# Transposing the queries and keys of the last sentence by DMA, not on TensorE, in a fused window-attention and mixture-of-experts kernel

## The chip, the cores and the metric

The kernel runs on one core of a Trainium2 chip. Its engines work side by side, each through its own instruction stream in order: TensorE (PE; loading its weights is shown apart as PEld), VectorE (DVE), ScalarE (ACT), GpSimd (POOL) and SyncE (SP). The metric is the device time of one execution in microseconds: 206.28 us, the median of three runs (205.09 to 207.0).

## The reference

Eight sentences of 576 positions, eight heads of 64. Attention looks back over a window of 64 positions; its output, averaged over the positions, picks one expert for the whole sentence, and a two-layer network of that expert is applied to every position.

```python
B, H, S, D = 8, 8, 576, 64
scores = q @ k^T / sqrt(D);  mask: 0 <= pos_q - pos_k < 64
attn   = softmax(scores);    x = (attn @ v) as [B, S, H*D = 512]
e      = argmax(x.mean(axis=1) @ w_gate)              # one of 8 experts per sentence
gate   = softmax(...)[e]
out    = gate * (relu(x @ w1[e]) @ w2[e])             # w1 512 x 1024, w2 1024 x 512
```

## The kernel before

Everything is written out as one list of steps, `OPS`: each entry is a letter, perhaps a letter for the engine (a for ACT, d for DVE, m for a PSUM tile out of the shared pool `ps_m`), and a number. A loop at the end of the kernel (L559 to L589) calls the function for each entry in turn, so that the list sets the order of the instructions on every engine, and of the DMA issues on each queue. An engine runs ahead of another as far as data and buffers allow. Sentences, heads and chunks are counted from 0.

*Attention.* A sentence has five units: 5b to 5b+3 are its four pairs of heads over positions 0 to 511 (a main unit), 5b+4 is the tail, positions 512 to 575 of all heads. Sentence 7 has the units 35 to 39. The steps of a unit:

- Q loads q or k of a whole sentence (`load_qk`, L104 to L112; Q14 and Q15 are sentence 7): one DMA on POOL's queue that casts to bf16. Partition p gets the positions 4p to 4p+3 of all heads, so that a piece of 256 elements is contiguous. t loads the tail of q and k (`load_tail`).
- T transposes on TensorE (`unit_tp`, L216 to L235): for a main unit 16 matmuls against the identity, 64 x 128 each, into a PSUM tile; for the tail 8.
- U copies the transposed queries out of PSUM into a tile `qt` (`unit_q`), k the keys into `kT` (`unit_kt`), on ACT or DVE. There are two `kT`, for even and odd sentences.
- S is the scores (L259 to L279), E the exp (ACT), K the mask (DVE), l the row sums by a matmul with ones, A the values (TensorE), n and R the reciprocal of the sums by ln and exp (ACT), X the normalisation (DVE).
- L loads v in tiles of 128 positions, V shifts a copy of it by 64 partitions (DVE).

*Gate.* g, j, G: after a sentence's last X a product on DVE, a small matmul (j, L394) and an argmax; P loads the index into a register of POOL, and W loads the expert's weights, four quarters of 512 KB (4b and 4b+1 are w1, 4b+2 and 4b+3 are w2, POOL's queue). Three weight buffers take turns; where the same expert lies in the buffer already, a load is skipped at run time.

*Experts.* c is the next of 144 chunks of TensorE's work, 18 a sentence: eight of w1 (`ph`, L465) and one of w1's tail (L472), eight halves of w2 (`po`, L524) and one of w2's tail (L533). A chunk is 8 matmuls over 512 columns, or 16 over 256. Chunk 18b is the first of sentence b; the chunk 18b+10 is the first to read the quarter W 4b+3. r empties a chunk's PSUM tile (ra on ACT, rd on DVE), B and D transpose the tail between the layers, O stores a result on POOL's queue, o on SP's. Stores run behind by up to 16 buffers.

*Queues.* All loads but the first two of q and k (SP) and the gate's matrix go through POOL's one DMA queue, at most eight under way; a load of that queue waits for the landing of the eighth before it. SP has no other work than its two first loads and the last stores.

Of the kernel before, what the change touches and what calls it, by code (L numbers as in the profile page):

```python
# [37 lines left out]
).split()  # L38

# [9 lines left out]
BF16 = mybir.dt.bfloat16  # L49
# [7 lines left out]
def kernel(  # L57
# [10 lines left out]
    nc = tc.nc  # L68
    B, H, S, D = q.shape
    Dm, E = moe_w_gate.shape  # L70
    F = moe_w1.shape[2]
    NP = H // 2
    NU = NP + 1
    SM = 512
# [3 lines left out]
    ld = ctx.enter_context(tc.tile_pool(name="ld", bufs=3))  # L78
    tpool = ctx.enter_context(tc.tile_pool(name="tpool", bufs=2))
    apool = ctx.enter_context(tc.tile_pool(name="apool", bufs=2))  # L80
# [23 lines left out]
    def load_qk(x, lohi):  # L104
        b, n = divmod(x, 2)
        tiles, src, tag = (qms, q, "qm") if n == 0 else (kms, k, "km")
        lo, hi = (int(lohi) // 10, int(lohi) % 10) if lohi else (0, H)
        if b not in tiles:
            tiles[b] = ld.tile([128, H, 256], BF16, tag=tag, name=tag)
        nc.gpsimd.dma_start(  # L110
            out=tiles[b][:, lo:hi],
            in_=src[b, lo:hi, 0:SM].rearrange("h (p r) d -> p h (r d)", r=4))  # L112

    raw = {}

# [91 lines left out]
    tT = {}  # L207
# [49 lines left out]
            copy(e)(out=kT[b % 2][:, :, 64 + SM:64 + S], in_=tp[:, :, 64:128])  # L257

    def unit_s(b, i, e):  # L259
        qt = tT.pop((b, i))  # L260
        kt = kT[b % 2]
        pm = 'b' in e
        if 'm' in e:
            sp = [ps_m.tile([128, 512], FP32, tag="mo", name="s") for _ in range(2)]
        else:
            s2 = ps_s.tile([128, 2, 512], FP32, tag="s", name="s")
            sp = [s2[:, 0], s2[:, 1]]
        n = 512 if i < NP else 256
        if pm:
            for hh in range(2):  # L270
                nc.tensor.matmul(out=sp[hh][:, 0:n], lhsT=ident, rhs=maskb if i < NP else masktb,
                                 start=True, stop=False, skip_group_check=True)
        for m in range(n // 64):
            for hh in range(2):
                p0 = 64 * hh
                kq = kt[p0:p0 + 64, i, 64 * m:64 * m + 128] if i < NP else kt[p0:p0 + 64, m, SM:SM + 128]
                nc.tensor.matmul(out=sp[hh][:, ts(m, 64)], lhsT=kq, rhs=qt[p0:p0 + 64, m],  # L277
                                 start=not pm, stop=True, skip_group_check=True)
        sps[b, i] = sp if 'm' in e else [s2[:, :, 0:n]]  # L279
# [278 lines left out]
    with tc.manual_schedule():  # L558
        for op in OPS:  # L559
# [17 lines left out]
                cast_raw(int(x.split(".")[0]), x.partition(".")[2], e)  # L577
            elif c == "W":
                load_w(int(x.split(".")[0]), x.partition(".")[2])
            elif c == "Q":  # L580
                load_qk(int(x.split(".")[0]), x.partition(".")[2])
            elif c in tail_ops:
# [37 lines left out]
```

## Time and profile before

| | |
|---|---|
| Median of three runs | 206.28 us |
| Profiled execution | 206.17 us, its span 204.6 us |
| PE busy | 189.6 us, 93% of the span |
| PEld, DVE, ACT, POOL busy | 57%, 60%, 65%, 53% |
| DMA | 39.02 MB in 81888 packets, 191 GB/s on average |

The span is the time from the first to the last instruction; the rest of the execution lies around it. Busy time is the union of an engine's instructions, so that pipelined matmuls overlap in it. In rows of groups, "x" is the count, then come busy us, mean ns of one, and the idle time of the engine just before with what ended it. The chain of waits is followed back from the last instruction.

### The profile page before, as it was taken

Reading aid. Unit: us, or ns where it says so; the run is one execution under the profiler, and the core shown is the slowest. Engines: PE = TensorE matmul, PEld = TensorE weight load, DVE = VectorE, ACT = ScalarE, POOL = GpSimd, SP = SyncE. Lnnn points to the kernel's source line nnn. Section 1 sums busy time; section 2 is a strip of 40 time slices with the busy share of each in tenths; the row PEclk is TensorE's granted clock in tenths of the full one; section 3 lists DMA queues with packets and bytes.
Section 4 is the critical chain, followed back from the end, with each engine's and each line's share of the span. In section 5 each row is a group of like instructions: output and inputs, shape, how many; then the busy total and the mean of one; then the engine's idle time right before and its main releaser. Section 6 shows DMA issues by size and latency. Waiting matters only on the chain.

```text
span 204.6 us, 7393 instructions
## 1 busy us (share of the span) xinstructions
PE 189.6 (93%) x3147; PEld 116.8 (57%) x3148; DVE 123.4 (60%) x351; ACT 133.6 (65%) x246; POOL 107.8 (53%) x157
## 2 busy tenths in 40 slices
PE   3886787999999999999999999999999899999992
PEld 1544544757576566666665666666565465556551
DVE  3587554798869746777447885877845257233210
ACT  3377795588988879498759697568587462403421
POOL 7996494423494654456531875099332570732610
PEclk9999996999999999999999999999999999999998
DMA  6999999999999999999999999999999472799923
GB/s 136 168 153 168 177 180 196 198 208 162 195 167 176 202 193 189 186 200 215 199 184 203 195 187 184 225 260 160 149 230 273 159 264 103 122 201 277 348 111 128
DMA packets 81888, 39.02 MB, mean 191 GB/s; under 512 B 48032, under 2 KB 79392, under 8 KB 81856
## 3 DMA queue, kind: packets, MB, share of 16 engines
q0 software_dynamic: 80192, 37.10, 130.7%
q1 hardware_dynamic: 1056, 1.38, 1.9%
q8 instruction: 24, 0.39, 0.7%
q10 hardware_dynamic: 608, 0.08, 0.3%
q14 instruction: 8, 0.07, 0.1%
HBM read 61.88 MB, written 9.44 MB: 349 GB/s over the span
## 4 chain that ended last, share of the span: by engine, by line
PE 70%; DMA 14%; POOL 5%; ACT 4%; issue 3%; DVE 1%; POOLq 1%; ACTq 0%
PE po L524 24%; PE ph L465 22%; DMA w2b<-in_moe_w_dram 8%; PE tp L227 5%; PE s L277 4%; DMA w1b<-in_moe_w_dram 3%; PE av L333 3%; PE po L533 3%; PE lb L311 3%; PE ph L472 3%; DMA qkt<-in_k_dram 2%; POOL vw L141 1%; POOL out_dram L513 1%; POOL qkt L133 1%; ACT rl L359 1%
## 5 line engine op out<-in xcount | busy, mean ns | idle before, releaser
L465 PE MATMUL ph<-xm,w1b 128*64 128x512 f16 x512 | 61.6, 385 | 1.8 <-DMA w1b<-in_moe_w_dram 1.8
L524 PE MATMUL po<-w2b,hm 128*64 128x512 f16 x512 | 61.4, 380 | 1.0 <-DMA w2b<-in_moe_w_dram 1.0
L465 PEld LDWEIGHTS <-w1b 128*64 128x64 f16 x512 | 27.7, 111 | 23.2 <-DMA w1b<-in_moe_w_dram 2.1
L524 PEld LDWEIGHTS <-hm 128*64 128x64 f16 x512 | 27.3, 110 | 21.8 <-issue 1.2
L451 ACT ACTIVATE hm<-ph,gw 128x512 f16<-128x512 f32 x35 | 24.2, 696 | 20.2 <-PE ph L465 20.1
L141 POOL DMA_DIRECT2D vw<-in_v_dram x32 | 28.7, 908 | 15.1 <-PE ph L465 4.8
L290 ACT ACTIVATE pe<-s 128x1024 f16<-128x1024 f32 x25 | 25.6, 1024 | 10.4 <-PE s L277 7.0
L353 ACT ACTIVATE ln<-lb 128x512 f32<-128x512 f32 (+1 forms) x40 | 22.5, 562 | 14.6 <-PE lb L311 11.7
L366 DVE CUSTOM_DVE_ANT_0 xm<-av,rl 128x512 f16<-128x512 f32 x32 | 21.9, 687 | 13.0 <-PE av L333 9.9
L453 DVE TENSOR_SCALAR hm<-ph,gw 128x512 f16<-128x512 f32 x29 | 21.1, 747 | 13.0 <-PE ph L465 12.7
L513 POOL DMA_DIRECT2D out_dram<-ob x29 | 16.2, 560 | 16.5 <-DMA vw<-in_v_dram 4.0
L359 ACT ACTIVATE rl<-ln 128x512 f32<-128x512 f32 (+1 forms) x40 | 23.3, 593 | 0.2
L299 DVE TENSOR_TENSOR pe<-pe,mask 128x1024 f16<-128x1024 f16 x28 | 18.9, 682 | 3.9 <-ACT pe L290 3.8
L503 DVE COPY ob<-po 128x512 f32<-128x512 f32 x13 | 9.0, 690 | 19.2 <-PE po L524 19.2
L503 ACT COPY ob<-po 128x512 f32<-128x512 f32 x19 | 11.2, 587 | 9.5 <-PE po L524 9.4
L428 POOL DMA_DIRECT2D w1b<-in_moe_w_dram x17 | 11.9, 698 | 10.2 <-PE ph L465 5.3
L333 PEld LDWEIGHTS <-vw 128*64 128x64 f16 x512 | 13.5, 115 | 5.9 <-DVE vw L151 0.6
L277 PEld LDWEIGHTS <-kT 64*128 64x128 bf16 x576 | 10.7, 96 | 9.7 <-issue 6.9
L227 PE MATMUL tp<-ident,qm 128*64 128x128 bf16 x256 | 13.2, 226 | 2.8 <-DVE qm L128 2.0
L333 PE MATMUL av<-pe,vw 128*64 128x64 f16 x512 | 14.6, 199 | 0.9 <-DVE vw L151 0.5
L311 PE MATMUL lb<-pe,ones 128*64 128x512 f16 x64 | 13.1, 392 | 1.7 <-ACT ln L353 1.3
L254 DVE COPY kT<-tp 128x512 bf16<-128x512 bf16 x19 | 12.8, 684 | 2.0 <-PE tp L227 2.0
(86 smaller groups left out, 265.6 us busy)
## 6 DMA issues: line engine op xcount, KB each, us to landing
w2b<-in_moe_w_dram POOLq DMA_DIRECT2D x16, 512.0 KB, 12.5
w1b<-in_moe_w_dram POOLq DMA_DIRECT2D x15, 512.0 KB, 9.5
out_dram<-ob POOLq DMA_DIRECT2D x29, 256.0 KB, 4.2
vw<-in_v_dram POOLq DMA_DIRECT2D x32, 128.0 KB, 9.1
km<-in_k_dram POOLq DMA_DIRECT2D x7, 512.0 KB, 11.1
qm<-in_q_dram POOLq DMA_DIRECT2D x7, 512.0 KB, 11.3
out_dram<-obt POOLq DMA_DIRECT2D x14, 64.0 KB, 4.2
out_dram<-ob SPq DMA_DIRECT2D x3, 256.0 KB, 2.3
```

The lines of the kernel that those rows point to most:

```text
L141: nc.gpsimd.dma_start(out=vt[:, 2 * J + 1], in_=v[b, :, 128 * J:128 * J + 128].rearrange("h c d -> c h d"))
L227: nc.tensor.transpose(tp[p0:p0 + 64, n, r], t[:, 2 * i + hh, ts(r, 64)], ident)
L290: nc.scalar.activation(out=po, in_=sp[0], func=AF.Exp, scale=scale)
L333: nc.tensor.matmul(out=av[p0:p0 + 64, :, 16 * m:16 * m + 16], lhsT=vt[:, m, 2 * i + hh], rhs=pe[:, hh, m], start=(m == 0), stop=(m == 7), ...
L353: nc.scalar.activation(out=ln, in_=lb[:, 0:n], func=AF.Ln)
L359: nc.scalar.activation(out=rl, in_=lns.pop((b, i)), func=AF.Exp, scale=-1.0)
L366: nc.vector.tensor_tensor_reduce(out=xm[:, i], in0=av.rearrange("q r p -> q (r p)"), in1=rl, scale=1.0, scalar=0.0, op0=ALU.mult, op1=ALU.add,
L451: nc.scalar.activation(out=o, in_=i, func=AF.Relu, scale=g)
L453: nc.vector.tensor_scalar(out=o, in0=i, scalar1=g, scalar2=0.0, op0=ALU.mult, op1=ALU.max)
L465: nc.tensor.matmul(out=ph[64 * c:64 * c + 64], lhsT=w1t[:, kb, ts(2 * ft + c, 64)], rhs=xm[:, kb], start=(kb == 0), stop=(kb == 3), skip_g ...
L503: copy(e)(out=ob, in_=po)
L524: nc.tensor.matmul(out=po[64 * c:64 * c + 64], lhsT=hm[:, fb, ts(2 * r + c, 64)], rhs=w2t[:, fb], start=(fb == 0), stop=(fb == 7), skip_gr ...
```

## The change

For sentence 7 alone, q and k of the positions 0 to 511 are loaded as eight row tiles, step N: one tile is 128 positions of all heads, 128 partitions with 8 pieces of 64 elements, POOL's queue, cast to bf16. N56 to N59 are q, N60 to N63 are k. A new step Z transposes a tile by a DMA that SP issues: Z56 to Z59 into a tile `qT`, for which the third of the `qm` buffers is taken, Z60 to Z63 straight into `kT`. Za7 and Zb7 do the same with the tail. The steps T, U and k of the units 35 to 39 are gone, and Q14, Q15 with them. The score matmuls of a main unit of sentence 7 read `qT` through a view that takes every fourth position, so that positions within a group stay in the order that the other sentences have; the columns that one matmul streams then lie 8 bytes apart.

The list of steps is the same up to its 367th entry, and in a new order from there on; what the other steps do is unchanged.

```diff
+    XB = (7,)
+    qTs = {}
+
+    def load_blk(x):
+        b, n, J = x // 8, x // 4 % 2, x % 4
+        tiles, src, tag = (qms, q, "qm") if n == 0 else (kms, k, "km")
+        if b not in tiles:
+            tiles[b] = ld.tile([128, 4, H, D], BF16, tag=tag, name=tag)
+        nc.gpsimd.dma_start(
+            out=tiles[b][:, J],
+            in_=src[b, :, 128 * J:128 * J + 128].rearrange("h c d -> c h d"))
+
+    def xpose(x):
+        b, n, J = x // 8, x // 4 % 2, x % 4
+        if n:
+            src, dst = kms[b], kT[b % 2][:, :, 64 + 128 * J:192 + 128 * J]
+        else:
+            if b not in qTs:
+                qTs[b] = ld.tile([128, NP, SM], BF16, tag="qm", name="qT")
+            src, dst = qms[b], qTs[b][:, :, 128 * J:128 * J + 128]
+        nc.sync.dma_start_transpose(out=dst, in_=src[:, J].rearrange("c h d -> c (h d)"))
+
+    def xpose_qt(b):
+        qt = apool.tile([128, NP, 64], BF16, tag="qtt", name="qtt")
+        nc.sync.dma_start_transpose(out=qt, in_=qkts[b][0:64].rearrange("c h d -> c (h d)"))
+        tT[b, NP] = qt
+
+    def xpose_kt(b):
+        nc.sync.dma_start_transpose(out=kT[b % 2][:, :, 64 + SM:64 + S],
+                                    in_=qkts[b][64:128].rearrange("c h d -> c (h d)"))
...
     def unit_s(b, i, e):
-        qt = tT.pop((b, i))
+        if b in XB and i < NP:
+            qt = qTs[b][:, i].rearrange("q (m p r) -> q m r p", m=8, r=4)
+        else:
+            qt = tT.pop((b, i))
...
+            elif c == "N":
+                load_blk(int(x))
+            elif c == "Z":
+                {"": xpose, "a": xpose_qt, "b": xpose_kt}[e](int(x))
```

SP's queue from its first load to its end, now (`raw` is the first q and k, `ob` and `obt` are results):

```order
L150 DMA raw<-in_q_dram 128x2x256
L150 DMA raw<-in_k_dram 128x2x256
L134 DMA_TRANSPOSE qT<-qm 128x4x128 x2
L134 DMA_TRANSPOSE kT_95<-km 128x4x128
L134 DMA_TRANSPOSE qT<-qm 128x4x128
L134 DMA_TRANSPOSE kT_95<-km 128x4x128
L134 DMA_TRANSPOSE qT<-qm 128x4x128
L134 DMA_TRANSPOSE kT_95<-km 128x4x128 x2
L138 DMA_TRANSPOSE qtt<-qkt 128x4x64
L142 DMA_TRANSPOSE kT_95<-qkt 128x4x64
L547 DMA out_dram<-ob 128x512 x2
L547 DMA out_dram<-obt 64x256
```

The ten transposes stand where nothing stood; in order they are Z56, Z57, Z60, Z58, Z61, Z59, Z62, Z63, Za7 and Zb7.

POOL's queue from the load of sentence 4's expert index (P4) on, before (`w1b_97` and `w2b_100` are that sentence's weights, `vw` is v, `qkt` a tail of q and k):

```order
L415 TENSOR_LOAD eidx
L133 DMA qkt<-in_q_dram 64x8x64
L133 DMA qkt<-in_k_dram 64x8x64
...
L428 DMA w1b_97<-in_moe_w_dram 128x4x512
L141 DMA vw_91<-in_v_dram 128x8x64 x4
...
L428 DMA w1b_97<-in_moe_w_dram 128x4x512
...
L431 DMA w2b_100<-in_moe_w_dram 128x4x512
L145 DMA vw_91<-in_v_dram 64x8x64
L513 DMA out_dram<-ob 128x512
```

and now, up to the last row tile (`qm` and `km` are the tiles of N57, then N61, N58, N59, N62 and N63):

```order
L449 TENSOR_LOAD eidx
L122 DMA qm<-in_q_dram 128x8x64
...
L462 DMA w1b_97<-in_moe_w_dram 128x4x512
...
L462 DMA w1b_97<-in_moe_w_dram 128x4x512
...
L465 DMA w2b_100<-in_moe_w_dram 128x4x512
...
L465 DMA w2b_100<-in_moe_w_dram 128x4x512
L122 DMA km<-in_k_dram 128x8x64
L122 DMA qm<-in_q_dram 128x8x64 x2
L122 DMA km<-in_k_dram 128x8x64
L547 DMA out_dram<-ob 128x512
L122 DMA km<-in_k_dram 128x8x64
```

The four weight quarters now stand closer behind the index, and five of the eight row tiles behind them; Q14 and Q15 stood ahead of the index. The loads of v of sentence 6 (four rows of `vw_91`) have moved: three ahead of the index, one between the w1 quarters (left out here with the two of `qkt`).

POOL's queue at sentence 7's expert index (P7), before:

```order
L513 DMA out_dram<-ob 128x512 x3
L415 TENSOR_LOAD eidx
L428 REGISTER_ALU x2
L428 ISA
L428 DMA w1b_97<-in_moe_w_dram 128x4x512
```

and now:

```order
L547 DMA out_dram<-ob 128x512 x4
L547 DMA out_dram<-obt 64x256 x2
L449 TENSOR_LOAD eidx
L547 DMA out_dram<-ob 128x512
L462 REGISTER_ALU x2
L462 ISA
L462 DMA w1b_97<-in_moe_w_dram 128x4x512
```

A store has come between the index and the first weight quarter. On TensorE the matmul of that gate (j7) stands behind 116 chunks and not 111, that of sentence 5 (j5) behind 78 and not 74, that of sentence 4 (j4) behind 61 and not 59, and the first score unit of sentence 7, S36 now, behind 89 chunks.

42 rows, old and new, of the table OPS are left out of this document.

## The prediction

> **What bounds the kernel now.** I read the table of stretches first, then the chain of waits, then TensorE's and POOL's instructions in order of time. The table of stretches (stretch and its length, busy us and instructions of PE, PEld, DVE, ACT and POOL, granted clock, DMA share, GB/s):
>
> ```profile
> 20.00:40.00 20.00, 16.19 (x343) 10.76 (x342) 11.38 (x35) 14.51 (x29) 12.87 (x16) 0.91 1.68 187
> 100.00:120.00 20.00, 20.00 (x378) 12.99 (x374) 14.57 (x44) 15.14 (x29) 8.34 (x11) 1.00 1.55 193
> 140.00:150.00 10.00, 10.00 (x190) 6.71 (x188) 7.94 (x24) 6.69 (x14) 5.12 (x8) 1.00 1.29 173
> 150.00:160.00 10.00, 9.17 (x100) 4.80 (x97) 3.88 (x12) 7.35 (x15) 2.78 (x6) 1.00 1.12 239
> 160.00:170.00 10.00, 9.87 (x160) 6.31 (x161) 5.29 (x19) 5.01 (x10) 6.46 (x15) 1.00 0.69 241
> ```
>
> From about 40 us on TensorE has no gap but the 0.83 and 0.13 us missing in the last two rows; no other engine is near full. Which wait makes that gap is told by the chain and by TensorE in order of time:
>
> ```profile
> PE 70%; DMA 14%; POOL 5%; ACT 4%; issue 3%; DVE 1%; POOLq 1%; ACTq 0%
> ```
> ```profile
> 143.63 16.46 DMA w2b<-in_moe_w_dram
> 160.13 1.05 PE po L524 x8
> ```
> ```profile
> 160.13 1.05 PE L524 MATMUL po<-w2b,hm 128*64 128x512 f16 x8 [0.96 <-DMA w2b<-in_moe_w_dram]
> ```
>
> Sentences are counted from 0. The second half of sentence 5's w2 (step W23, issued at 143.63) lands 16.46 us later, and TensorE waits 0.96 us for it. So there are two things to win: TensorE's own work, one us for one us, and this wait.
>
> **The change part by part.** *Transposes removed.* TensorE in order of time (start, busy):
>
> ```profile
> 123.37 0.39 PE L227 MATMUL tp<-ident,qm 128*64 128x128 bf16 x8
> 123.59 0.39 PE L227 MATMUL tp<-ident,km 128*64 128x128 bf16 x8
> 123.81 0.38 PE L311 MATMUL lb<-pe,ones 128*64 128x512 f16 x2
> 127.18 0.41 PE L234 MATMUL tpt<-ident,qkt 128*64 128x128 bf16 x8
> 127.43 1.04 PE L533 MATMUL po<-w2b,ht 128*64 128x256 f16 x16
> 128.30 1.89 PE L465 MATMUL ph<-xm,w1b 128*64 128x512 f16 x16
> ```
>
> From start to next start a main transpose step takes 123.81 - 123.37 = 0.44 us, the tail one 127.43 - 127.18 = 0.25. Four and one leave: 4 x 0.44 + 0.25 = 2.0 us off a full TensorE. At some places the chain has more for one:
>
> ```profile
> 68.16 0.57 PE tp L227 x16
> ```
>
> By that it would be 2.5 us; I take 2.0. The ten copies that empty their PSUM tiles leave DVE and ACT too; I cost that at nothing, since both lie under TensorE's work (14.57 and 15.14 of 20 us).
>
> *Score matmuls of the last sentence* now read the queries with a step of 8 bytes, not densely. Their present cost:
>
> ```profile
> 122.14 0.41 PE L277 MATMUL s<-qt,kT 64*128 64x64 bf16 x16
> 122.48 1.05 PE L524 MATMUL po<-w2b,hm 128*64 128x512 f16 x8
> ```
>
> 0.34 us a unit. No row shows a stepped read of a moving operand; at worst it doubles, 4 x 0.34 = +1.4 us; a gain is excluded, as the columns are as many. The row-sum matmul writes its output in a stepped order and still takes what the dense ones do (392 against 385 ns in the groups below), so I take 0.
>
> ```profile
> L465 PE MATMUL ph<-xm,w1b 128*64 128x512 f16 x512 | 61.6, 385 | 1.8 <-DMA w1b<-in_moe_w_dram 1.8
> L311 PE MATMUL lb<-pe,ones 128*64 128x512 f16 x64 | 13.1, 392 | 1.7 <-ACT ln L353 1.3 <-ACT pe L290 0.2
> L141 POOL DMA_DIRECT2D vw<-in_v_dram x32 | 28.7, 908 | 15.1 <-PE ph L465 4.8 <-DMA qm<-in_q_dram 3.1 <-DMA w1b<-in_moe_w_dram 2.1
> L110 POOL DMA_DIRECT2D qm<-in_q_dram x9 | 7.9, 881 | 6.4 <-issue 2.7 <-PE lb L316 2.4 <-POOLq L604 0.8
> ```
>
> *Loads.* Eight row-tile loads (N) replace two whole ones (Q14, Q15). On POOL: 8 x 0.91 - 2 x 0.88 = +5.5 us, where POOL is busy for half the span. On the DMA engines an N load has the shape of a v load (1024 pieces of 64 elements). Traffic in three stretches, in this order 123 to 125 us (nearly all v), 100 to 101.5 (all q), 176 to 183 (all weights):
>
> ```profile
> DMA packets 2191, 0.33 MB, mean 163 GB/s; under 512 B 2142, under 2 KB 2190, under 8 KB 2190
> DMA packets 587, 0.30 MB, mean 198 GB/s; under 512 B 7, under 2 KB 587, under 8 KB 587
> DMA packets 1395, 1.41 MB, mean 202 GB/s; under 512 B 32, under 2 KB 1394, under 8 KB 1394
> ```
>
> 1024 small pieces at 2142 in 2 us are 0.96 us, a whole q load (0.52 MB at 198 GB/s) 2.65, a weight quarter (0.52 MB at 202) 2.6. So 8 x 0.96 - 2 x 2.65 = +2.4 us of DMA time: little.
>
> *DMA transposes (Z)* run on SP, which has nothing else from its two first loads to the last stores. Nothing in the trace is a DMA transpose. Nearest rows of DMA issues (KB each, us to landing):
>
> ```profile
> out_dram<-ob SPq DMA_DIRECT2D x3, 256.0 KB, 2.3
> raw<-in_k_dram SPq DMA_DIRECT2D x1, 256.0 KB, 3.3
> vw<-in_v_dram POOLq DMA_DIRECT2D x32, 128.0 KB, 9.1
> ```
>
> So 2.3 to 9.1 us for one of 128 KB; I take 3.3, the slower of the two on SP's own queue, with several under way at once. The Trainium skill (DMA: Bandwidth & Descriptors, "Latency and other measured facts") gives DMA transposes an effective 261 GB/s; by it one would move for an estimated 0.5 us, and no transpose would be late; no run here shows it yet.
>
> The first reader is S36, which needs all eight. When is it due? Ahead of it TensorE has 89 chunks, as ahead of step 89 before (the tail w2 of sentence 4), and 4 transpose, 2 score, 1 value and 1 row-sum units fewer.
>
> ```profile
> 148.01 1.04 PE L533 MATMUL po<-w2b,ht 128*64 128x256 f16 x16
> 111.40 0.29 PE L394 MATMUL gps<-grd,ones 128*64 128x8 f32 x4
> 171.66 0.23 PE L394 MATMUL gps<-grd,ones 128*64 128x8 f32 x4
> ```
> ```profile
> 113.10 0.90 POOL L133 DMA_DIRECT2D qkt<-in_q_dram  x1 [4.84 <-DVE vw L150]
> 114.67 0.77 POOL L428 DMA_DIRECT2D w1b<-in_moe_w_dram  x1
> 173.66 1.62 POOL L428 DMA_DIRECT2D w1b<-in_moe_w_dram  x2 [5.31 <-PE ph L465]
> ```
>
> 148.01 - 4 x 0.44 - 2 x 0.34 - about 0.5 = 145.1 us. When are the tiles there? The gate of sentence 4 (j4, 111.40) has the same units and two chunks more ahead of it: a chunk is 0.86 us (6.91 / 8, row below), so 113.1. POOL went on 1.7 us after it (113.10); now it issues N57 at 114.8 and W16 at 115.7. Behind W16 the one DMA ring has to move four weight quarters (10.4), six N (5.8), a v load and two small q/k tails (2), a store (about 0.9): 19.1 us. How long from issue to traffic: the ring was empty when w1 was issued at 173.66, and the DMA share of the stretch 175.5 to 176.9 us in 40 slices of 0.035 us is
>
> ```profile
> DMA  0000055000189999989987999999987999999987
> ```
>
> busy steadily from the twelfth slice on, 175.9: 2.2 us. With 1 us of backlog and 1.5 to landing N63 is there at 115.7 + 2.2 + 1 + 19.1 + 1.5 = 139.5, N58, with three N and the store behind it (3.8), at 135.7. So Z63 may take 145.1 - 139.5 = 5.6 us if transposes overlap; one after another the last five (58, 61, 59, 62, 63) may take (145.1 - 135.7) / 5 = 1.9 each. With 3.3 and overlap: no wait.
>
> *Steps moved.* Sentence 5's weights (W20 to W23) now follow their gate with one v load among them, where four v loads, two q/k tails and four stores stood ahead. But the gate comes later: G5 stands behind 81 chunks, by the same count from 148.01 less 8 x 0.86, 4 x 0.44 and about 2.9 of other units, 136.5.
>
> ```profile
> 140.32 0.76 POOL L428 DMA_DIRECT2D w1b<-in_moe_w_dram  x1
> ```
>
> Gate to weight issue was about 1.6 us at sentence 7 (of the 2.0 below), and a store stands between now: W20 at 138.6, not 140.32. From there W23 landed 160.13 - 140.32 = 19.8 us later; with a ring empty but for the four (2.2 + 10.4), the v load and stores (1 + 1.5) it would be 15.1. So it lands between 153.7 and 158.4, middle 156.0. Its reader, step 100, came at 159.17 without the wait and comes 2.5 us earlier (2.0 of transposes and 0.5 of units moved behind it): 156.7. The 0.96 us goes, by 0.7.
>
> The gate of sentence 7 (j7) stands behind 116 chunks instead of 111, which shortens its lead over that sentence's first w1 matmul (185.10):
>
> ```profile
> 185.10 6.91 PE ph L465 x64
> 192.87 6.04 PE po L524 x56
> ```
> ```profile
> DMA to landing us min/median/max: 8.0/9.1/9.5
> ```
>
> j7 comes at 171.66 - 0.96 - 2.0 + 5 x 0.86 = 173.0; POOL issued 2.0 us after it (171.66 to 173.66), plus one store of 0.55 now: 175.6 and, for the second half, 176.4. The first matmul is due at 185.10 - 2.96 = 182.1, the second half 4 x 0.86 later, 185.6. By 8.0 to landing, the quiet figure (the row, for w1 after 100 us), the second half is there at 184.4; the first, 2.6 us of traffic ahead of it, at 181: margins of 1.1 and 1.2, no wait.
>
> **The sum.** 206.17 (profiled execution: span 204.6 and 1.6 around it; the median is 206.28) - 2.0 - 0.96 = 203.2. At two places (W23, w1 of sentence 7) the margin is about 1 us; I charge half of the 0.96 that such a place cost before: 203.7. Against the median that is 1.2% less.
>
> **The rivals.** *Slower: transposes one after another on SP.* If each starts only when the one ahead has landed, the point is 1.9 us; from 2.9 on the kernel is slower. At 3.3 the last is there at 135.7 + 5 x 3.3 = 152.2, TensorE stands 7.1 us and everything behind it too: 203.2 + 7.1 = 210.3; after an idle TensorE the clock may fall as well (0.91 over 20 us, first row quoted: 1.8 us), 212.1. For it: SP's queue is in order and no row shows its throughput; against: DMAs of POOL overlap (two w1 halves issued within 1.62 us were both there after 8.0). The Trainium skill (VectorE: DVE Perf Modes, "The three transpose paths") gives 1309 ns for one 128x128 block by DMA, over three times TensorE's; a transpose here has four blocks, so by it an estimated 5.2 us, the last at 161.7 and the time 219.8; no trace here shows it. Chance 0.21.
>
> *Waits take the gain.* If w1 of sentence 7 lands after 9.1 us for the first half, as the median of the row has it and not with an idle ring, it is there at 184.7: 2.6 us late, 205.8. W23 at the late end of its span keeps 1.7 us of wait: 204.9. For it: margins of 0.7 to 1.2 us out of sums that may be 2 us off. Against: the ring was empty from 171 to 175.9. Chance 0.21.
>
> *The work leaves TensorE and the time does not follow*, because copies and PSUM tiles set the pace under a TensorE that only looks full: then 206.2 - 0.96 = 205.2, or no change. Against: DVE 14.57 and ACT 15.14 of 20 us. Chance 0.08. The forecast keeps 0.50.
>
> **How the numbers follow.** One per cent, about what a measurement of this kernel can tell from no change, is 204.2 and 208.3. Forecast (203.2 to 204.2): faster, 0.50. Second and third rival: within, 0.29. First: slower, 0.21. The range goes down to 202.2 (a transpose step worth 0.57 us and half a us of spread), and up to 210.5, over the second and third rival and the near end of the first; left out are transposes of more than 3.3 us each in a row, and the clock's fall.
>
> **What would show it.** TensorE's transposes on main tiles fall from 512 to 448, and its busy time by about 2 us. S36's first weight load shows no wait for a DMA transpose, and those land within 5 us (rival one: several us of wait there, each landing behind the one before). No wait on w2b at sentence 5's second w2 half. No wait on w1b when sentence 7 starts (rival two). I would be wrong, too, if the stepped score matmuls of the last sentence took 0.6 us.

## The result

The changed kernel takes 219.99 us (median of four runs, 219.19 to 221.1), the kernel before beside it 205.78 (205.09 to 207.0). The ratio is 1.0688, with a 95% interval of 1.0612 to 1.0763: 7% slower, where 1% faster was forecast. The profiled execution took 219.64 us, with a span of 218.1.

The waits of TensorE in the changed kernel (total us, times, longest):

```profile
PE s L311 <- DMA kT<-km: 12.5, 3, 6.3
...
PE po L558 <- ACT ob L537: 1.3, 1, 1.3
```

Both rows are new, and the first is nearly the whole loss; the two left out belong to the start of the kernel. No row names w2b, the wait that the prediction wanted gone. The same waits on TensorE in order of time, from S36 on:

```profile
145.07 0.28 PE L311 MATMUL s<-qT,kT 64*128 64x64 bf16 x4
150.88 0.29 PE L311 MATMUL s<-qT,kT 64*128 64x64 bf16 x4 [5.53 <-DMA kT<-km]
157.49 0.29 PE L311 MATMUL s<-qT,kT 64*128 64x64 bf16 x4 [6.32 <-DMA kT<-km]
158.43 0.29 PE L311 MATMUL s<-qT,kT 64*128 64x64 bf16 x4 [0.65 <-DMA kT<-km]
```

S36 is reached at 145.07; the forecast said 145.1. There is luck in the match: this execution happened to be 1.9 us ahead of the one forecast from (below), and lost 1.31 us to a wait at L558 just ahead of S36. It then stands three times, once for each of the last three key tiles: 12.5 us. SP's issues of the transposes from Z58 on, and from the chain of waits the piece that S36 waits for last:

```profile
136.46 1.24 SPq L134 DMA_TRANSPOSE qT<-qm  x1
137.80 1.59 SPq L134 DMA_TRANSPOSE kT<-km  x1
139.49 2.29 SPq L134 DMA_TRANSPOSE qT<-qm  x1
141.89 5.76 SPq L134 DMA_TRANSPOSE kT<-km  x2
```
```profile
145.82 12.56 DMA kT<-km
```

The tiles were there nearly when they were forecast (Z58 is issued at 136.46, forecast 135.7; the last tile, N63, was issued at 128.50 and landed 12.2 us later, at 140.7, forecast 139.5), but the transposes take long, twice over: SP is held 1.2 to 3.8 us by the issue of one (5.76 for the last two), so that the last is issued about 145.8, and it is under way until 158.4. Here is the traffic of 115 to 160 us: POOL's queue (q0) and SP's (q1) with packets, MB and the time that their packets took as a share of 16 engines, then issues with their median us to landing:

```profile
q0 software_dynamic: 15456, 6.71, 130.0%
q1 hardware_dynamic: 4352, 1.05, 26.1%
...
out_dram<-ob POOLq DMA_DIRECT2D x5, 256.0 KB, 10.3
...
qT<-qm SPq DMA_TRANSPOSE x4, 9.3
kT<-km SPq DMA_TRANSPOSE x4, 12.8
```

So a transpose lands 9.3 us (queries) or 12.8 (keys) after its issue, the medians of four, and single ones after 7.4 to 15.6, where 3.3 were taken. Issue and landing together put the last five at about 145.3, 150.8, 154.0, 157.5 and 158.4. A transpose moves in packets of about 256 bytes (4352 for the 1.05 MB of eight). While they run, POOL's queue moves 6.71 MB; in the same 45 us of the kernel before, it moved 9.13:

```profile
q0 software_dynamic: 18310, 9.13, 138.6%
```

Stores of 256 KB now take 10.3 us to land in the median of five (7.2 in the kernel before, of ten). One of them is late for a buffer that ACT needs, which is the 1.3 us at L558 in the list of waits. The table of stages (TensorE's busy time is the first pair behind the length; the granted clock stands behind the five engines):

```profile
20.00:40.00 20.00, 17.44 (x391) 11.68 (x392) 14.25 (x42) 16.85 (x34) 12.53 (x15) 1.00 1.66 186
140.00:150.00 10.00, 4.37 (x48) 2.57 (x47) 3.95 (x16) 3.86 (x8) 4.25 (x7) 1.00 1.38 135
150.00:160.00 10.00, 2.15 (x26) 1.57 (x28) 0.00 (x0) 1.24 (x2) 3.70 (x5) 0.53 1.36 176
160.00:170.00 10.00, 10.00 (x128) 5.56 (x126) 5.64 (x11) 5.04 (x8) 0.00 (x0) 0.79 1.02 97
```

After the long idling the clock is halved, by these means from 150.6 to 164.2. Work done at half clock is from 158.6 on: 160 to 170 loses 10 x 0.21 = 2.1 us, the stretch before it 0.7, together 2.8. Between 20 and 40 us the clock is 1.00 where the execution before had 0.91 after a wait that this one does not have; the steps there are the same, so that is the executions' own spread; at the end of the common steps this one is some 1.9 us ahead (the same chunk begins at 76.34 us, and at 78.24 before).

The span grew by 13.5 us: 12.5 (S36) + 1.3 (store) + 2.8 (clock) + 0.8 (stepped reads, below) - 2.0 (transposes gone) - 0.96 (w2b) - 1.9 (spread) = 12.5. One us is left unexplained.

### The profile page after: what moved, and what is told of

Same layout as the page of the kernel before. It is cut to its first block, busy times and chain, and to the rows that moved or that the text cites. A ratio compares the mean times of both kernels' runs of the same rounds, so it can differ in the third digit from the quotient of the medians.

```text
span 218.1 us, 7268 instructions
## 1 busy us (share of the span) xinstructions
PE 191.1 (88%) x3075; PEld 118.9 (55%) x3076; DVE 125.5 (58%) x352; ACT 128.7 (59%) x234; POOL 113.3 (52%) x164
## 4 chain that ended last, share of the span: by engine, by line
PE 56%; DMA 29%; POOL 6%; issue 2%; DVE 2%; ACT 2%; POOLq 1%; SPq 0%; DVEq 0%; ACTq 0%
PE ph L499 19%; PE po L558 19%; DMA vw<-in_v_dram 9%; DMA out_dram<-ob 7%; DMA kT<-km 6%; DMA w1b<-in_moe_w_dram 5%; DMA qkt<-in_q_dram 4%; PE po L567 3%; PE s L311 3%; PE av L367 3%; PE tp L258 2%; PE lb L345 2%; PE ph L506 2%; POOL vw L172 1%; POOL qm L110 1%
## 5 line engine op out<-in xcount | busy, mean ns | idle before, releaser
L558 PE MATMUL po<-w2b,hm 128*64 128x512 f16 x512 | 61.3, 379 | 1.3 <-ACT ob L537 1.3
L499 PE MATMUL ph<-xm,w1b 128*64 128x512 f16 x512 | 62.4, 385 | 0.0
L324 ACT ACTIVATE pe<-s 128x1024 f16<-128x1024 f32 x26 | 26.6, 1023 | 27.2 <-PE s L311 22.3
L558 PEld LDWEIGHTS <-hm 128*64 128x64 f16 x512 | 29.5, 110 | 21.2 <-issue 1.6
L499 PEld LDWEIGHTS <-w1b 128*64 128x64 f16 x512 | 28.4, 112 | 20.8 <-issue 1.2
L547 POOL DMA_DIRECT2D out_dram<-ob x30 | 16.9, 565 | 34.1 <-DVE pe L333 14.7
L485 ACT ACTIVATE hm<-ph,gw 128x512 f16<-128x512 f32 x32 | 22.1, 692 | 15.9 <-PE ph L499 15.3
L487 DVE TENSOR_SCALAR hm<-ph,gw 128x512 f16<-128x512 f32 x32 | 23.7, 748 | 7.8 <-PE ph L499 7.0
L311 PEld LDWEIGHTS <-kT 64*128 64x128 bf16 x576 | 11.6, 97 | 25.0 <-DMA kT<-km 13.0
L367 PEld LDWEIGHTS <-vw 128*64 128x64 f16 x512 | 12.8, 113 | 4.4 <-DVE vw L182 0.6
L258 PE MATMUL tp<-ident,qm 128*64 128x128 bf16 x224 | 12.0, 230 | 2.5 <-DVE qm L159 2.1
L285 DVE COPY kT<-tp 128x512 bf16<-128x512 bf16 x18 | 12.2, 685 | 3.5 <-PE tp L258 3.5
```

Of the source, the lines that this page charges most:

```text
L324: nc.scalar.activation(out=po, in_=sp[0], func=AF.Exp, scale=scale)
L367: nc.tensor.matmul(out=av[p0:p0 + 64, :, 16 * m:16 * m + 16], lhsT=vt[:, m, 2 * i + hh], rhs=pe[:, hh, m], start=(m == 0), stop=(m == 7), ...
L485: nc.scalar.activation(out=o, in_=i, func=AF.Relu, scale=g)
L487: nc.vector.tensor_scalar(out=o, in0=i, scalar1=g, scalar2=0.0, op0=ALU.mult, op1=ALU.max)
L499: nc.tensor.matmul(out=ph[64 * c:64 * c + 64], lhsT=w1t[:, kb, ts(2 * ft + c, 64)], rhs=xm[:, kb], start=(kb == 0), stop=(kb == 3), skip_g ...
L558: nc.tensor.matmul(out=po[64 * c:64 * c + 64], lhsT=hm[:, fb, ts(2 * r + c, 64)], rhs=w2t[:, fb], start=(fb == 0), stop=(fb == 7), skip_gr ...
```

## The experiments

**First question: is it the wait, the transposes' traffic, the row tiles, or the new order?** The first run takes S36's wait away and leaves all else: sentence 7's main scores read a constant tile with the same step, and the keys of sentence 6, so nobody reads the tiles that are still loaded and transposed.

```diff
+    cq = const.tile([128, SM], BF16)
+    nc.vector.memset(cq, 0.0625)
...
-            qt = qTs[b][:, i].rearrange("q (m p r) -> q m r p", m=8, r=4)
+            qt = cq.rearrange("q (m p r) -> q m r p", m=8, r=4)
...
-        kt = kT[b % 2]
+        kt = kT[0 if b in XB and i < NP else b % 2]
```

> Loads and DMA transposes stay, but the score matmuls of sentence 7's main units read a constant tile and sentence 6's keys, so that nothing waits for a transpose (sentence 7's scores are left out). Theory, the wait at S36 is the loss: its 12.5 us and the 2.8 us of half clock behind it go, 219.99 - 15.3 = about 205. Rival, the transposes' traffic and the new order cost of themselves: above 209.

Measured: 211.41 us, ratio 1.029 (1.0232 to 1.0349). The wait explains 1.0688 - 1.029 = 0.040, or 8.2 us of 205.6, the clock's fall included. That is about half of the 15.3 us that the theory gave it: where S36 does not stand, other waits come in its place. The kernel is still slower than before though nobody waits for a transpose. TensorE in order of time shows where, and the traffic of 115 to 160 us shows why:

```profile
141.85 1.92 PE L560 MATMUL po<-w2b,hm 128*64 128x512 f16 x16 [0.70 <-ACT ob L539]
151.87 3.64 PE L501 MATMUL ph<-xm,w1b 128*64 128x512 f16 x32 [2.94 <-DVE obt L544]
162.52 1.05 PE L560 MATMUL po<-w2b,hm 128*64 128x512 f16 x8 [0.86 <-DMA w2b<-in_moe_w_dram]
169.86 0.29 PE L313 MATMUL s<-qtt,kT 64*128 64x64 bf16 x8 [1.53 <-DMA kT<-qkt]
```
```profile
q0 software_dynamic: 15615, 6.64, 126.5%
q1 hardware_dynamic: 4352, 1.05, 27.9%
...
w1b<-in_moe_w_dram POOLq DMA_DIRECT2D x4, 512.0 KB, 13.0
w2b<-in_moe_w_dram POOLq DMA_DIRECT2D x4, 512.0 KB, 15.2
```

Two waits are for output buffers whose store has not landed, one for w2, one for the tail's own transpose: 6.0 us together.

Next, the transposes are left out, and then the row tiles too (each on top of the first run):

```diff
-Z56 ... Z57 Z60 ... Z58 Z61 ... Z59 Z62 ... Z63
```

> The changed kernel with the eight whole transposes of sentence 7 left out altogether; its twelve score units of rows 0 to 511 read a constant tile (same stepped pattern) and the keys of sentence 6, so sentence 7's queries and keys of those rows are not used; the row-tile loads stay. Against the run that kept the transposes but waited for none of them (211.41), this is the price of their traffic alone. Theory (the transposes slow the store of out and the weights packet by packet): the waits for the store's buffer (2.94) and for w2b (0.86) go, and the time falls by 3 to 4 us, to 207 to 208.5. Rival (what was left of the loss, 5.6 us, is the new order and the stepped reads): it stays within 1 us of 211.4.

```diff
-Z56 ... Z63
-N60 ... N56 ... N57 ... N61 N58 ... N59 ... N62 ... N63
```

> The same, with the eight row-tile loads of sentence 7 left out too, so that only the tail's loads and transposes are left of sentence 7's queries and keys: the price of the row-tile loads alone, and below it what order and stepped reads cost. Theory (their 1 MB costs DMA time that nobody waits for): within 0.7 us of the kernel with the loads; 206.5 to 208. Rival (the loads delay the weights behind them on GpSimd's queue, as the old order with the loads showed): 2 us or more faster than with the loads, 205 to 206.

Measured: 203.26 us without the transposes, ratio 0.986 (0.9788 to 0.9931); 204.12 without the row tiles too, 0.9874 (0.9801 to 0.9947). The traffic of the eight transposes alone, with nobody waiting, costs 0.043, or 8.8 us. That is more than its theory's 3 to 4 us. The row tiles cost nothing that can be told (0.0014, uncertain by 0.01). In the kernel without transposes the traffic of 115 to 160 us reads:

```profile
q0 software_dynamic: 19857, 8.43, 138.6%
...
w1b<-in_moe_w_dram POOLq DMA_DIRECT2D x4, 512.0 KB, 8.6
w2b<-in_moe_w_dram POOLq DMA_DIRECT2D x4, 512.0 KB, 10.7
```

POOL's queue moves 8.43 MB instead of 6.64, the same eight quarters of weights land after 8.6 and 10.7 us instead of 13.0 and 15.2, and from 100 us to the end TensorE has no wait in this trace. This is also the forecast's kernel but for the disputed step, and it has the forecast's time: 203.7 was said (the ratio is uncertain by 0.007, 1.5 us).

**Is it the order?** One kernel keeps the new order with TensorE's transposes put back, another keeps the old order with row tiles and DMA transposes.

```diff
-    XB = (7,)
+    XB = ()
...
-N60 W15 N56 ... N57 ... N61 N58 ... Z58 ... Z59 Z62 ... Z63
+Q15 W15 Q14 ... T36 ... kd36 Ua36 ... T35
```

> The new order alone: sentence 7 loaded whole and transposed on TensorE as before, its steps put where the row loads and DMA transposes stood. Theory, the order is not the loss: within 1.5% of before, 204 to 208, with the wait of 0.96 us for sentence 5's w2 gone. Rival, the order itself costs: over 209.

```diff
-Q14 L29 Q15
+N56 N57 N58 N59 L29 N60 N61 N62 N63
...
-Tm35
+Z56 Z57 Z58 Z59 Z60 Z61 Z62 Z63
...
-T39
+Za7 Zb7
```

> The DMA transposes alone: the old order, row tiles in place of Q14 and Q15 (ahead of sentence 4's expert index), all eight transposes in place of the first transpose of sentence 7. Theory, late row tiles and the weights beside them made them late: here the tiles are there by about 125 and the first reader comes near 137, no wait for a transpose, 203.5 to 206. Rival, 4.4 to 5.2 us each in a row: 8 of them from about 112 take 35 to 42 us, the reader waits 10 us or more, above 215.

Measured: 208.62 us, 1.0194 (1.0124 to 1.0264), for the order with TensorE's transposes; 218.6, 1.0596 (1.0518 to 1.0674), for the old order with DMA transposes. The waits on TensorE, first of the former, then of the latter:

```profile
PE htp L521 <- ACT qt L274: 1.8, 1, 1.8
PE po L557 <- DMA w2b<-in_moe_w_dram: 1.5, 1, 1.5
```
```profile
PE ph L498 <- DMA w1b<-in_moe_w_dram: 6.1, 3, 2.9
```

The first comes out a little over its theory's 1.5%, and the wait for w2b, which was to go, is 1.5 us. It is no clean measure of the order: its 1.8 us come from where I put the copies back. That the new order need not cost anything is shown by the run without transposes, at 0.986. The second is clean in one thing. In the old order nobody waits for a transpose, and there is a loss all the same: 6.1 us of waits for w1, and the clock falls behind them (0.66 between 130 and 140 us). The eight row tiles stand ahead of that w1 too, so this run does not tell their part from the transposes'. A loss is there in either order; the order decides who waits.

**Second question: why do the transposes land late?** Sentence 5's weights, loaded at the same time, are left out:

```diff
-Am34 c W20 O n34 ... X34 W21 W22 L38 ... A31 W23 E35
+Am34 c O n34 ... X34 L38 ... A31 E35
```

> The weights of sentence 5 (W20 to W23, 2 MB, issued beside the last five transposes) aren't loaded; sentence 5 uses what lies in the buffer. Theory, a transpose is slow because its packets take turns with the weights' on the DMA engines: the last five land within 3 to 6 us of issue each, S36 waits under 4 us, about 208. Rival, a transpose takes 4.4 to 5.2 us by itself and they go one after another: the last one still lands near 158 and S36 still waits 10 us or more, about 218.

Measured in a single run: 212.5 us. S36 waits 5.8 us instead of 12.5, and the transposes land after 6.9 and 7.6 us instead of 9.3 and 12.8. It is between the two theories: the weights beside them are about half of the wait.

The transpose by itself, in the kernel before, issued late in the program out of sentence 7's result (nobody reads it):

```diff
-X39
+X39 Z0 Z1 Z2 Z3 Z4 Z5 Z6 Z7
...
+            elif c == "Z":
+                t, j = divmod(int(x), 4)
+                if j == 0:
+                    tps["z"] = ld.tile([128, 4, 4, 128], FP16, tag="qm", name="zz")
+                nc.sync.dma_start_transpose(out=tps["z"][:, j], in_=xs[7][0][:, j])
```

> The kernel before, with eight DMA transposes of the same shape (128 x 512 bf16, out of a row tile of sentence 7 into a buffer that nobody reads) issued on SyncE's queue behind X39, where GpSimd's queue has nothing left to load; everything else is computed as before. It measures the transpose by itself. Theory (beside GpSimd's loads each engine takes one packet of either ring in turn, and a transpose has 512 of them): each occupies SyncE about 1.2 us and lands 3 to 4 us after its issue. Rival (a transpose takes 4.4 to 5.2 us one after another by its nature, so eight take 35 to 42 us): the eight land one after another, each 4 us or more behind the one before.

Here are SP's issues of three of the eight, and each one's us to landing:

```profile
165.50 1.22 SPq L581 DMA_TRANSPOSE zz<-xm  x1
166.85 1.28 SPq L581 DMA_TRANSPOSE zz<-xm  x1
168.30 1.82 SPq L581 DMA_TRANSPOSE zz<-xm  x1
```
```profile
zz<-xm SPq DMA_TRANSPOSE x1, 3.8
zz<-xm SPq DMA_TRANSPOSE x1, 4.0
zz<-xm SPq DMA_TRANSPOSE x1, 3.1
```

With only stores on POOL's queue, a transpose holds SP for 1.2 to 1.8 us and lands after 3.1 to 4.0. The three land at about 169.3, 170.9 and 171.4, no more than 1.5 us apart. So here transposes overlap, and the 3.3 us taken in the prediction are about right for this place. The rival, 4.4 us or more one after another by nature, falls. Over all eight the landing takes 2.5 to 9.0 us, median 3.9; the first (7.3) and the last (9.0) have loads of weights beside them. In a second profile of the same kernel it is 3.1 to 11.0, median 5.5. The next expectation is for this kernel's time:

> The kernel before with eight more DMA transposes behind X39 (one look so far: 203.77 beside 206.15), now timed. Theory (a transpose costs time only where the loads that it delays are on the path): within 1% of the kernel before. Rival (each costs 1 us wherever it stands): 4 to 8 us slower.

Measured: 204.67 us, 0.9967 (0.9929 to 1.0004). Eight transposes cost nothing that can be told at this place.

**Third question: is it the transposing, or the packets?** In the first run's kernel, where nobody waits, each transpose becomes a plain copy of the same 128 KB: to the same places in 512 pieces of 256 bytes, or in 128 pieces of 1 KB.

```diff
-        nc.sync.dma_start_transpose(out=dst, in_=src[:, J].rearrange("c h d -> c (h d)"))
+        nc.sync.dma_start(out=dst, in_=src[:, J].rearrange("c (p h) d -> c p (h d)", h=2))
```

> As the run that kept the transposes but waited for none of them (211.41), with each of the eight whole transposes turned into a plain copy of the same 128 KB to the same place, 512 runs of 256 bytes, untransposed; sentence 7's queries and keys of rows 0 to 511 are not used. Without any of these transfers the kernel took 203.26, so their traffic cost 8.1 us. Theory (it is the number of packets that GpSimd's ring has to take turns with): the copy costs the same, 209.5 to 212. Rival (transposing itself is what keeps the engines): the copy costs less than 3 us, below 206.5.

```diff
-        nc.sync.dma_start_transpose(out=dst, in_=src[:, J].rearrange("c h d -> c (h d)"))
+        dst = kT[b % 2][:, J, 64:64 + SM] if n else qTs[b][:, J]
+        nc.sync.dma_start(out=dst, in_=src[:, J].rearrange("c h d -> c (h d)"))
```

> The same with plain copies of 128 runs of 1 KB (a quarter of the packets, the same bytes). Theory (packets): about a quarter of the 8.1 us, 205 to 206. Rival (transposing itself): the same as with the short copies, both below 206.5. Rival (bytes): the same as with the transposes, 209.5 to 212.

Measured: 205.6 us, 1.0005 (0.9964 to 1.0047), and 204.33, 0.9968 (0.9934 to 1.0002). My theory (the number of packets) falls for the larger part: the same packets without transposing cost 0.0145 over none, 3.0 us, and with transposing another 0.0285, 5.9 us. The long copies, a quarter of the packets, cost 0.0108, 2.2 us; that is too near to the short ones to show that the number of packets sets a price. Then the short copies in the changed kernel itself, where S36 waits for them:

> The changed kernel with its eight whole transposes turned into plain copies of 512 runs of 256 bytes to the same places, and sentence 7's scores wait for them and read them as they are (rows not transposed, so sentence 7's scores of rows 0 to 511 are not those of the reference). Theory A (the late landing comes from taking turns with GpSimd's ring, 512 turns a copy, as the short copies landed after 8.6 and 13.0 us): S36 still waits 5 to 11 us, and the time is 210 to 215. Theory B (the transposing makes both the traffic and the landing slow): S36 waits less than 3 us, below 207.

Measured: 214.7 us, 1.0414 (1.0317 to 1.051). The waits on TensorE, and the traffic of 115 to 160 us:

```profile
147.21 0.28 PE L311 MATMUL s<-qT,kT 64*128 64x64 bf16 x4 [1.11 <-DMA kT<-km]
153.50 0.29 PE L311 MATMUL s<-qT,kT 64*128 64x64 bf16 x4 [6.02 <-DMA kT<-km]
154.77 0.29 PE L311 MATMUL s<-qT,kT 64*128 64x64 bf16 x4 [0.98 <-DMA kT<-km]
```
```profile
q1 hardware_dynamic: 4292, 1.07, 16.0%
...
qT<-qm SPq DMA_DIRECT2D x4, 128.0 KB, 7.9
kT<-km SPq DMA_DIRECT2D x4, 128.0 KB, 12.7
```

Here the theory of taking turns holds: plain copies land as late as the transposes (7.9 and 12.7 us against 9.3 and 12.8), and S36 waits 8.1 us for them. The copies of 1 KB pieces, a quarter of the packets, landed much sooner:

```profile
qT<-qm SPq DMA_DIRECT2D x4, 128.0 KB, 5.6
kT<-km SPq DMA_DIRECT2D x4, 128.0 KB, 6.7
```

The turns can be counted. Here are the packets of POOL's queue (q0) and SP's (q1) in the changed kernel from 151 to 154 us, while S36 waits:

```profile
q0 software_dynamic: 479, 0.48, 93.1%
q1 hardware_dynamic: 474, 0.11, 29.6%
```

One for one, 158 a us for SP: at that pace the 512 packets of one transpose take 3.2 us, and those behind it on the queue come after it. The Trainium skill (DMA: Bandwidth & Descriptors, "Queues, rings and completion order") says that each DMA engine goes round the queues that it has work for, one packet at a time, where a packet of the page can hold several descriptors. The equal counts, and the landings of short and long copies, agree with it.

The five kernels, as ratios to the kernel before:

| | nobody waits | S36 waits |
|---|---|---|
| nothing in their place | 0.986 | |
| plain copies, 512 packets each | 1.0005 | 1.0414 |
| transposes, 512 packets each | 1.029 | 1.0688 |

The two steps add up in either order: transposing costs 0.0285 or 0.0274, waiting 0.041 or 0.040. Each difference is uncertain by about 0.01, 2 us. In time: 3.0 us for the plain copies, 5.9 for the transposing, 8.2 for the wait.

One trace of the transposing is the mean time that a packet takes an engine (share x 16 engines x 45 us / packets): 43 ns in the changed kernel (26.1%, 4352), 46 in the first run (27.9%, 4352), 27 for the plain copies (16.0%, 4292). The mean is not the common packet: in the 3 us shown above, with transposes, it is 30 ns. By the first run's packet records, 104 of 4608 packets of 256 bytes took over 100 ns each, and these hold a third of the time; with plain copies in the changed kernel 9 of 4608 did. What holds these few is not shown. The shares of the queues overlap, so this cannot be turned into us of the span.

**Is the price per transpose?** Half of them, the keys', nobody waiting:

```diff
         else:
+            return
             if b not in qTs:
```

> As the run that kept the eight transposes but waited for none of them (211.41), with only the keys' four left (the queries' four are left out; sentence 7's queries and keys of rows 0 to 511 are not used). With none it took 203.26. Theory (every transpose takes about 1 us of DMA time from loads that are on the path): about half of the 8.1 us, 206.5 to 208.5. Rival (the loss comes from one unlucky meeting with a store or a weight, not from each): 204.5 or less, or 210 or more.

Measured: 204.96 us, 0.9967 (0.9924 to 1.0009): 2.2 us over none, between the theory's band and the rival's. So the price is not even: four cost 2.2 us, the other four 6.6, each uncertain by under 2 us. In this kernel TensorE has no wait for a store or a weight between 115 and 166 us. My reading is that four fit into the slack that loads and stores have, and eight don't; the runs do not show that slack apart.

**Does another place help?** All row tiles and transposes earlier:

```diff
-L24 Dd2 I3
+L24 N56 N57 N58 N59 N60 N61 N62 N63 Dd2 I3
...
-S25 g4
+S25 Z56 Z57 Z58 Z59 Z60 Z61 Z62 Z63 g4
```

> The changed kernel with the eight row-tile loads moved ahead, right behind L24 (before P3), and all eight transposes right behind S25, so that they are issued some 15 us earlier; nothing else moved, everything computed. Theory (the transposes take long only beside GpSimd's loads, and the wait at S36 is a matter of when they are issued): the 12.5 us at S36 and the clock fall after them go, some 1 to 4 us come back as waits for w1 and w2 of sentences 3 and 4; 206 to 211. Rival (the transposes take their 7 to 15 us at any place and block what shares the engines): the same transposes now stand in front of the weights of sentence 4, and the loss only moves, 214 or more.

Measured: 216.5 us, 1.0475 (1.0377 to 1.0574). S36 does not wait any more, but:

```profile
113.83 1.92 PE L498 MATMUL ph<-xm,w1b 128*64 128x512 f16 x8 [9.11 <-DMA w1b<-in_moe_w_dram]
```

The row tiles stand ahead of that sentence's w1 on POOL's queue and the first four transposes beside it (issued from 100.82), and the loss moves there; which of the two delays that w1 is not told apart. The rival had the time right.

**Two smaller ones.** The stepped read, with the first run's constant queries read densely:

```diff
-            qt = cq.rearrange("q (m p r) -> q m r p", m=8, r=4)
+            qt = cq.rearrange("q (m t) -> q m t", m=8)
```

> As the run that kept the transposes but waited for none of them, with the constant queries read densely instead of in steps of four elements (sentence 7's queries and keys of rows 0 to 511 are not used). It measures the stepped read alone. Forecast (the step is free): a score unit of sentence 7 takes the same 0.6 us and the time stays at 211.4. Rival (the changed kernel's trace, 0.55 us for 16 matmuls against 0.34): the unit falls by 0.2 us, 0.8 us in all, 210.6.

A unit and the instruction behind it, stepped (first run) and dense:

```profile
145.95 0.61 PE L313 MATMUL s<-cq,kT 64*128 64x64 bf16 x16
146.49 1.06 PE L569 MATMUL po<-w2b,ht 128*64 128x256 f16 x16
```
```profile
148.11 0.41 PE L313 MATMUL s<-cq,kT 64*128 64x64 bf16 x16
148.45 1.06 PE L569 MATMUL po<-w2b,ht 128*64 128x256 f16 x16
```

0.54 us stepped, 0.34 dense: 0.2 for each of four units, 0.8 us. The time of the single run, 212.69 us, is too coarse to show it.

The other tries to win the 0.96 us of w2b in the kernel before by itself, with sentence 5's weights right behind their gate:

```diff
-P5
+P5 W20 W21 W22 W23
```

> The kernel before with one move: the loads of sentence 5's weights W20 to W23 stand right behind P5 on GpSimd's queue instead of among sentence 7's steps. Everything is computed. Theory: the wait of 0.96 us for w2b goes and nothing else is late, a ratio of 0.995. Rival: the loads move in front of other loads and stores of GpSimd's queue and these are waited for instead, a ratio of 1.0 or more.

Measured: 215.66 us, 1.049 (1.0444 to 1.0537). The wait for w2b is gone, but the v loads now stand behind the weights: DVE waits for one, and the gate stands behind that on DVE:

```profile
154.05 0.69 DVE L149 COPY vw<-vw 64x2048 f16<-64x2048 f16 x1 [9.09 <-DMA vw<-in_v_dram]
```
```profile
PE gps L393 <- DVE grd L385: 7.9, 1, 7.9
```

No complete kernel tried here beats the kernel before.

## Why the prediction was wrong

The step that failed is the one on the transposes: "So 2.3 to 9.1 us for one of 128 KB; I take 3.3", and "With 3.3 and overlap: no wait". They land after 9.3 to 12.8 us, and S36 waits 12.5. Both halves of it failed at this place.

The 3.3 us are about right for a quiet place (3.1 to 4.0 measured). But at 136 to 145 us POOL's queue is full, and there the row of the v loads, 9.1 us for 128 KB in short pieces, was the nearest, though it is another queue: the first of the last five landed after 8.8. With that row the wait would have been 139.5 + 9.1 - 145.1 = 3.5 us and the time 207.2: no gain, but still not the size.

The rest is the overlap. "With several under way at once" is so, as 137.80 is issued long before 136.46 has landed, but it does not bring them in soon after one another. The tiles of the last five were forecast within 3.8 us (135.7 to 139.5); their transposes land 5.5, 3.2, 3.5 and 0.9 us apart, 13.1 in all, 3.3 on average, near the 3.2 us that 512 packets need at the pace counted above. The sum had no term for this, and none for SP's own issues: the last transpose was forecast to be issued at 139.5 and land at 142.8; it was issued at 145.8, 5.1 us after its tile was there, and landed at 158.4. Why the issues took longer than the 1.2 us of a quiet place is not shown, nor how much an earlier one would have helped, since the one ahead landed only at 157.5.

A second hole has no row that I could have misread: the prediction worked out 2.4 us of DMA time for the row tiles and none for the transposes. What they take from weights and stores costs 8.8 us (3.0 for the moving, 5.9 for the transposing) with nobody waiting for them. In the changed kernel these waits are mostly not seen beside S36's: w2b and the tail's transpose have none there. The first rival didn't have this either.

The other steps, by the runs:

- *Transposes removed, -2.0, and w2b's wait, -0.96:* borne out as a sum, within 1.5 us. The kernel without the DMA transposes takes 203.26 us; 203.7 was forecast.
- *S36 due at 145.1:* 145.07, with luck, as said with the result. *Row tiles:* Z58 was issued at 136.46, forecast 135.7; the loads cost nothing that can be told.
- *No wait on w1b when sentence 7 starts:* held, so the second rival did not come. One margin there was worked out wrong: 184.4 - 2.6 is 181.8 and not 181, so that the first half had 0.3 us and not 1.1. Nothing came of it.
- *Stepped reads at nothing:* wrong, 0.8 us, inside the bound of +1.4.
- *The first rival, one after another on SP:* the side is right, and so was its remark that the clock may fall (2.8 us, 1.8 said). Beside the full queue it is also nearest in mechanism: they land in order, 3.3 us apart on average, which is its 3.3, though by chance, as that came from a plain load; its last landing, 152.2, is 6.2 us early mostly because the first took 8.8. But it is no property of SP's queue alone, since the three of the quiet run land at most 1.5 us apart. The time that the Trainium skill's figure gave beside it, 219.8 us, is within 0.2 of the result, and its last landing, 161.7, is 3.3 us off. I would not take that as the figure's merit: the same page (VectorE: DVE Perf Modes, "The three transpose paths") has one price for a block, and the runs show one transpose of four blocks at 2.5 us and at 15.6.
- *261 GB/s, by the Trainium skill (DMA: Bandwidth & Descriptors, "Latency and other measured facts"), an estimated 0.5 us each:* no landing agrees; the shortest, in the quiet run, is 2.5 us. A landing holds more than the moving: from 170 to 171 us of that run SP's queue moved 675 packets, and at this pace the 512 of one transpose take an estimated 0.76 us. The Trainium skill also says (Advanced Engine Details and Errata, "X-Bar Transpose (TRN2)"): "TRN2 transpose DMAs are as fast as regular DMAs". The landings of transposes and of plain copies with the same packets agree with that beside a full queue; the cost to other queues' traffic, 5.9 us, does not.
- *The range* left out "transposes of more than 3.3 each in a row", though the bounds of the step reached to 9.1. It did hold the row of 9.1 us with overlap (207.2); nothing in it stood for the traffic.

## What to carry to other kernels

A transfer takes as long as the queues beside it make it: take its duration from a row of the same piece size and the same stage, not of the same queue. Several of them on one queue, beside another that is full, land one behind the other, so add them up. A DMA that hides on an idle queue still takes turns on engines that others need, so it needs a term in the sum for what it delays, above all where weights and stores already arrive just in time; here eight transposes saved TensorE 2.0 us and cost the kernel 8.8 before anyone waited for them. Before moving such a transfer elsewhere, ask which load stands there: earlier, a loss came up as a 9.11 us wait for w1; behind sentence 7's attention, they cost nothing that can be told.

## What was not expected of the hardware

- A DMA transpose of 128 x 512 bf16 took 1.2 us of SP's queue to issue even when quiet; a plain copy of the same bytes took half of that in its shortest issues, beside a busy POOL queue:

```profile
137.97 0.60 SPq L134 DMA_DIRECT2D kT<-km  x1
```

- Its packets of 256 bytes take an engine 46 ns on average beside other traffic, 27 ns without transposing; a few long ones make the difference (104 of 4608 over 100 ns, against 9).
- While POOL's queue and SP's both had work, they moved packets one for one, 479 and 474 in 3 us, though POOL's were four times as large (0.48 MB against 0.11).
- Queries read in steps of 8 bytes made a score unit take 0.54 us instead of 0.34, though the columns are as many.
